# GeGLU feed-forward on one core: gate/up tiles in pairs, two plain tiles in place of four, and part of the seven-product work done in the head

## The chip, the core and the metric

The kernel runs on one core of one Trainium2 chip. The metric is the device time of one execution in microseconds (us), as a median of several executions. Each execution is fast or slow, by its time. The profile is a trace of one execution. It covers the span of that execution, from its first to its last instruction, which is 1.7 to 2.1 us shorter than the timed run. In this kernel the matmuls write to PSUM, in banks, and all other tiles lie in SBUF. A load has landed when its data are there. Engines: PE is TensorE (matmuls), PEld its weight loads, DVE is VectorE, ACT is ScalarE, POOL is GpSimd, SP is SyncE, which issues most DMAs.

## The reference

```python
B, S, D, F = 32, 32, 1024, 3584          # bf16; x has 1024 tokens
def reference(x, w_gate, w_up, w_down):
    return (gelu_tanh(x @ w_gate) * (x @ w_up)) @ w_down
```

## The kernel before

The 1024 tokens fall into two halves of 512, d_model into a front and a rear half of 512, and the 3584 features into 28 tiles of 128. Gate and up projection of a tile can be computed in two ways:

- *plain*: gate and up, two token halves, 8 matmuls each: 32 matmuls, all in bf16;
- *seven products* (Strassen-Winograd over [gate, up] and the two token halves): 7 products of 4 matmuls, so 28 matmuls. Two of the seven (a11·b11 and a12·b21, the second called P2) are bf16. The other five take sums of weights (s1 to s4, or a22 cast) and sums of x (t1 to t4, or b22 cast) in fp32r, a 32-bit type.

The kernel before computes four tiles plain, because that can start as soon as the first quarter of x and of the weights is there. It computes the other 24 with seven products, one tile at a time. GpSimd forms s1 to s4 of the next two tiles meanwhile. The down projection is a second seven-product scheme, of 392 matmuls.

```python
    # b11, b12: front half of d_model for the first, second 512 tokens; b21, b22: rear half
    FC = 2; F0 = 4                                  # four plain tiles in the head
    def acc(tag): ...                               # one PSUM bank; A 3, B 2, C 2, G 1 of them
    # [cut: loads in quarters of d_model, plain tiles for the first and then the second tokens]

        open_ft = None
        ahead = first_product(F0)                   # a11 * b11 into a bank of A, copied out ("sn1")
        for ft in range(F0, FT):                    # one tile at a time
            # [cut: start GpSimd's sums of the next pair and the loads of the one after]
            (psa, sn1), psc, psb = ahead, acc("C"), acc("B")
            prod(psc, s1, t1, True)
            sn5 = snap(psc, "sn5", 2)               # copy PSUM to SBUF on ScalarE
            # [cut: GpSimd's next sum]
            prod(psa, s2, t2, False)
            sn2 = snap(psa, "sn2", 1)
            # [cut: a22 of a later tile cast to fp32r, on ScalarE]
            if open_ft:
                last_product(open_ft)               # a22r * t4 of the tile before
            prod(psc, s4, b22r, False)
            c12 = added(sn2, psc)                   # VectorE add
            h1 = acc("G")                           # gelu's result in PSUM
            nc.scalar.activation(h1, c12, ACT.Gelu_apprx_tanh)
            prod(psb, quads(ci, fl)[1], b21, True)  # P2
            c11 = added(sn1, psb)
            h0 = ework.tile([P, NB], bf16, name="h", tag="h")
            nc.scalar.activation(h0, c11, ACT.Gelu_apprx_tanh)
            # [cut: GpSimd's next sum]
            if ft + 1 < FT:
                ahead = first_product(ft + 1)
            prod(psa, s3, t3, False)
            c22 = added(sn5, psa)
            tt(g_of(ft)[:, NB:], c22, h1, MUL)
            open_ft = (ft, psa, h0)
```

## Time and profile before

| | before |
|---|---|
| median time | 277.13 us (276.96 to 277.27, 3 runs) |
| span of the trace | 275.2 us |
| start / head / loop / down projection / tail | 4.4 / 29.0 / 149.7 / 88.4 / 3.6 us |

The page's first part (busy time and its share of the span) and its fourth (the chain of work that ended last):

```profile
PE 270.1 (98%) x1190; PEld 184.3 (67%) x1207; DVE 173.1 (63%) x184; ACT 114.4 (42%) x179; POOL 94.9 (34%) x51
...
PE 98%; issue 0%; ACT 0%
```

TensorE is busy nearly always and the chain never leaves it. But the Trainium skill warns in "Perfetto Trace Analysis", section "Identifying the Most-Contended Engine", that busy time of pipelined matmuls is a poor measure of how near the limit they run. So I look at the distance between starts. The timeline of before (start, length, engine, line, operation, tiles, count):

```profile
18.93 1.89 PE L221 MATMUL psA<-b,wg 128*128 128x512 bf16 x8
20.66 1.89 PE L221 MATMUL psB<-b,wu 128*128 128x512 bf16 x8
...
40.92 1.07 PE L268 MATMUL psA<-t,a22r 128*128 128x512 f32 x4
41.82 1.07 PE L268 MATMUL psC<-b22r,s 128*128 128x512 f32 x4
...
45.39 1.08 PE L268 MATMUL psC<-t,s 128*128 128x512 f32 x4
...
51.69 1.08 PE L268 MATMUL psC<-t,s 128*128 128x512 f32 x4
```

Eight bf16 matmuls take 20.66 - 18.93 = 1.73 us, 0.216 us each; four fp32r matmuls take 0.90 us, 0.227 us each once the starts are taken to the nanosecond. A tile of the loop should therefore need 20 × 0.227 + 8 × 0.216 = 6.27 us. The s1·t1 groups of four start at 45.39, 51.69 and 57.99 us, 6.30 us apart. So there is nothing to win in the loop but 0.03 us a tile, unless matmuls go. In what follows a loss "by starts" is the distance between two starts beyond this spacing.

The time by stretch (each row: stretch, its length, then the busy time of each engine with its instruction count, the granted clock, the DMA share and GB/s). The stretches are the head up to the first s1·t1 product, the loop up to the first matmul of the down projection, and the down projection:

```profile
core 0: us, PE busy (x) PEld busy (x) DVE busy (x) ACT busy (x) POOL busy (x), PEclk, DMA share, GB/s
4.38:33.42 29.04, 28.93 (x131) 12.82 (x132) 15.22 (x15) 9.23 (x13) 0.00 (x0) 1.00 0.89 213
33.42:183.14 149.72, 148.90 (x654) 105.74 (x665) 84.04 (x120) 82.30 (x142) 94.16 (x45) 1.00 0.29 80
183.14:271.55 88.41, 88.25 (x394) 64.12 (x396) 73.31 (x49) 20.59 (x22) 0.00 (x0) 1.00 0.51 167
```

Two groups of VectorE instructions will matter later: the multiplies by h1 (second token half, h1 in PSUM), for the two halves of the feature tiles. In such a line, after the shapes and the count, come the busy time and the mean nanoseconds of one:

```profile
L331 DVE TENSOR_TENSOR hi<-c,psG 128x512 bf16<-128x512 f32 x14 | 9.7, 690 | 1.8 <-DVE c L284 0.4
L331 DVE TENSOR_TENSOR lo<-c,psG 128x512 bf16<-128x512 f32 x10 | 6.9, 689 | 1.5 <-DVE c L284 0.5
```

### The profile page before, as it was taken

Reading aid. Unit: us, or ns where it says so; the run is one execution under the profiler, and the core shown is the slowest. Engines: PE = TensorE matmul, PEld = TensorE weight load, DVE = VectorE, ACT = ScalarE, POOL = GpSimd, SP = SyncE. Lnnn points to the kernel's source line nnn. Section 1 sums busy time; section 2 is a strip of 40 time slices with the busy share of each in tenths; the row PEclk is TensorE's granted clock in tenths of the full one; section 3 lists DMA queues with packets and bytes.
Section 4 is the critical chain, followed back from the end, with each engine's and each line's share of the span. In section 5 each row is a group of like instructions: output and inputs, shape, how many; then the busy total and the mean of one; then the engine's idle time right before and its main releaser. Section 6 shows DMA issues by size and latency. Waiting matters only on the chain.

```text
span 275.2 us, 3268 instructions
## 1 busy us (share of the span) xinstructions
PE 270.1 (98%) x1190; PEld 184.3 (67%) x1207; DVE 173.1 (63%) x184; ACT 114.4 (42%) x179; POOL 94.9 (34%) x51
## 2 busy tenths in 40 slices
PE   8999999999999999999999999999999999999995
PEld 3444467766677777777666777754447888888883
DVE  0049975555555555555555555556999999999511
ACT  4034455555555555555555555430200022972001
POOL 1000059996766749494947660000000000000000
PEclk9999999999999999999999999999999999999999
DMA  7999023150505143250508500003992245786202
GB/s 150 323 248 270 2 76 96 59 155 0 155 0 152 26 126 87 68 137 17 152 2 249 171 2 1 0 0 126 335 337 82 91 166 169 245 270 209 77 0 76
DMA packets 52192, 33.77 MB, mean 123 GB/s; under 512 B 8656, under 2 KB 52176, under 8 KB 52176
## 3 DMA queue, kind: packets, MB, share of 16 engines
q1 hardware_dynamic: 49184, 30.94, 39.1%
q10 hardware_dynamic: 2992, 2.62, 3.0%
q8 instruction: 9, 0.15, 0.2%
q14 instruction: 7, 0.06, 0.1%
HBM read 29.62 MB, written 2.10 MB: 115 GB/s over the span
## 4 chain that ended last, share of the span: by engine, by line
PE 98%; issue 0%; ACT 0%
PE psA L268 31%; PE psC L268 16%; PE psA L352 14%; PE psB L268 7%; PE psB L352 7%; PE psC L352 7%; PE psG L352 5%; PE psA L221 4%; PE psC L221 3%; PE psB L221 3%; PE psG L205 1%; PE psG L221 1%; PE tp L213 0%; ACT o_sb L491 0%; PE psG L217 0%
## 5 line engine op out<-in xcount | busy, mean ns | idle before, releaser
L268 PE MATMUL psA<-t,s 128*128 128x512 f32 x192 | 56.2, 414 | 0.0
L268 PEld LDWEIGHTS psA<-t,s 128*128 128x128 f32 x192 | 36.1, 188 | 9.4 <-ACT sn L279 0.2
L156 POOL TENSOR_TENSOR s<-wu 128x1024 fp32r<-128x1024 bf16 x11 | 23.7, 2150 | 29.3 <-PE psC L268 29.3
L284 DVE TENSOR_TENSOR c<-sn,psA 128x512 f32<-128x512 f32 x24 | 16.6, 690 | 25.4 <-PE psA L268 25.4
L268 PEld LDWEIGHTS <-wg 128*128 128x128 bf16 x192 | 16.9, 98 | 23.3 <-issue 6.3
L279 ACT COPY sn<-psA 128x512 f32<-128x512 f32 x48 | 27.8, 579 | 10.4 <-PE psA L268 10.4
L268 PE MATMUL psC<-t,s 128*128 128x512 f32 x96 | 26.1, 394 | 0.0
L268 PE MATMUL psA<-t,a22r 128*128 128x512 f32 x96 | 25.9, 391 | 0.0
L320 ACT ACTIVATE psG<-c 128x512 f32<-128x512 f32 x24 | 14.4, 602 | 27.4 <-DVE c L284 27.4
L268 PE MATMUL psC<-b22r,s 128*128 128x512 f32 x96 | 25.6, 389 | 0.0
L268 PE MATMUL psA<-b,wg 128*128 128x512 bf16 x96 | 24.6, 379 | 0.0
L158 POOL TENSOR_TENSOR s<-wg,s 128x1024 fp32r<-128x1024 bf16 x11 | 23.8, 2165 | 0.9
L157 POOL TENSOR_TENSOR s<-s,wg 128x1024 fp32r<-128x1024 f32 x11 | 23.5, 2137 | 0.9
L159 POOL TENSOR_TENSOR s<-wg,wu 128x1024 fp32r<-128x1024 bf16 x11 | 23.5, 2139 | 0.0
L268 PE MATMUL psB<-b,wg 128*128 128x512 bf16 x84 | 22.2, 381 | 0.8
L279 ACT COPY sn<-psC 128x512 f32<-128x512 f32 x24 | 14.1, 589 | 20.3 <-PE psC L268 20.3
L290 DVE TENSOR_TENSOR hi<-h,psA 128x512 bf16<-128x512 bf16 x14 | 9.6, 689 | 19.8 <-PE psA L268 19.8
L268 PEld LDWEIGHTS psC<-t,s 128*128 128x128 f32 x96 | 18.0, 188 | 4.3
L268 PEld LDWEIGHTS psA<-t,a22r 128*128 128x128 f32 x96 | 18.0, 188 | 3.8
L268 PEld LDWEIGHTS psC<-b22r,s 128*128 128x128 f32 x96 | 17.9, 188 | 3.8 <-ACT sn L279 0.2
L284 DVE TENSOR_TENSOR c<-sn,psC 128x512 f32<-128x512 f32 x24 | 16.5, 689 | 5.0 <-PE psC L268 5.0
L284 DVE TENSOR_TENSOR c<-sn,psB 128x512 f32<-128x512 f32 x24 | 16.5, 687 | 2.8
(99 smaller groups left out, 420.5 us busy)
## 6 DMA issues: line engine op xcount, KB each, us to landing
wg<-in_w_gate_dram SPq DMA_DIRECT2D x12, 512.0 KB, 4.0
wu<-in_w_up_dram SPq DMA_DIRECT2D x12, 512.0 KB, 5.2
wdb<-in_w_down_dram SPq DMA_DIRECT2D x12, 512.0 KB, 4.7
wdb<-in_w_down_dram SPq DMA_DIRECT2D x12, 384.0 KB, 4.2
v<-in_w_down_dram SPq DMA_DIRECT2D x4, 512.0 KB, 6.9
out_dram<-o_sb ACTq DMA_DIRECT2D x16, 128.0 KB, 1.7
v<-in_w_down_dram SPq DMA_DIRECT2D x4, 384.0 KB, 7.6
wg<-in_w_gate_dram SPq DMA_DIRECT2D x3, 256.0 KB, 3.9
```

Source lines behind the costliest of these rows:

```text
L156: yield eng.tensor_tensor(s1, a21, a22, ADD)
L157: yield eng.tensor_tensor(s2, s1, a11, SUB)
L158: yield eng.tensor_tensor(s4, a12, s2, SUB)
L159: yield eng.tensor_tensor(s3, a11, a21, SUB)
L205: nc.tensor.matmul(warm_ps, lhsT=ones_w, rhs=ones_m, start=True, stop=True)
L221: nc.tensor.matmul(ps, lhsT=w_tiles[0][which][:, dt, fl * P : (fl + 1) * P], rhs=x_rows(dt, nb), start=(dt == 0), stop=(dt == DT - 1),)
L268: nc.tensor.matmul(ps, lhsT=lhs[:, k, :], rhs=rhs[:, k, :], start=(start and k == 0), stop=(k == KD - 1), skip_group_check=True,)
L279: nc.scalar.copy(t, ps)
L284: tt(t, s, ps, ADD)
L290: tt(g_of(ft)[:, :NB], h0, psa, MUL)
L320: nc.scalar.activation(h1, c12, ACT.Gelu_apprx_tanh)
L352: nc.tensor.matmul(banks[m], lhsT=lhs(k)[:, m * P : (m + 1) * P], rhs=rhs(k), start=(start and k == 0), stop=(k == HF - 1), skip_group_che ...
```

## The change

The intent is to have only two plain tiles, so that 26 tiles instead of 24 use 28 matmuls in place of 32. Then the head would be too short to cover the loading of x, of the weights and the forming of t1 to t4. So ten P2 products (a12·b21) of later tiles are pulled into the head. They need nothing but the rear half of d_model for the first tokens; therefore the head works on that half first. Their results wait in SBUF, in room that the second half of the gated activations takes later. Besides, the loop now handles two tiles together, product by product.

```diff
-    F0 = 4
-    NCH = (FT - F0) // FC + 1
+    NCH = FT // FC
+    NAHEAD = 10
 ...
+        # head: first half of the reduction of 4 ahead products, then of the 2 plain tiles, ...
+        for k in range(KQ):
+            for j in range(KB):
+                product_ahead(ps[j], 0, j, k, k + 1)
+        plain0(KD, KD + KQ)
+        for j, copy in enumerate((nc.scalar.copy, nc.vector.tensor_copy) * 2):
+            product_ahead(ps[j], 0, j, KQ)
+            copy(ahead[0][:, j, :], ps[j])
+        plain0(KD + KQ, DT)
+        # [cut: loads; 4 more ahead products]
+        tt(t1, b12, b11, SUB)
+        for fl in range(FC):                       # front half of the first tokens
+            for which in (0, 1):
+                plain(tok0[fl][which], which, fl, 0, 0, KD, KD, KD - 1)
+            plain_out(fl, 0, *tok0[fl])
+        tok1 = [(acc("A"), acc("B")) for _ in range(FC)]     # second tokens
+        # [cut: their matmuls; t2, three sums; 2 more ahead products]
 ...
+            if ft < FC + NAHEAD:                   # in first_product
+                return psa, gelu(added(ahead_of(ft), psa), "h0", 4)
 ...
-        for ft in range(F0, FT):
+        for ci in range(1, NCH):                   # one pair of tiles
+            # [cut: GpSimd's sums and the loads; fts is the pair, psa its banks of A]
+            psc = [acc("C") for _ in fts]
+            for fl in range(FC):
+                prod(psc[fl], s1[fl], t1, True)
+                sn5.append(snap(psc[fl], "sn5"))
+            for fl in range(FC):
+                prod(psa[fl], s2[fl], t2, False)
+                sn2.append(snap(psa[fl], "sn2"))
+            for st in open_fts:
+                last_product(st)
+            for fl, ft in enumerate(fts):
+                prod(psc[fl], s4[fl], b22r, False)
+                h1.append(gelu(added(sn2[fl], psc[fl]), "h1", 2))    # h1 now bf16 in SBUF
+                a22r_of(ft)
+            # [cut: P2 of both tiles where it was not done ahead]
+            begun = [first_product(ft + FC) for ft in fts] if ci + 1 < NCH else []
+            for fl, ft in enumerate(fts):
+                prod(psa[fl], s3[fl], t3, False)
+                tt(g_of(ft)[:, NB:], added(sn5[fl], psa[fl]), h1[fl], MUL)
```

PSUM banks are dealt anew (A 4, B 2, C 2; G is gone).

More of the change, by code (lines that the diff above doesn't have):

```diff
@@ L68 @@
     ring = ctx.enter_context(tc.tile_pool(name="ring", bufs=4))
-    opool = ctx.enter_context(tc.tile_pool(name="osb", bufs=4))
     one = ctx.enter_context(ExitStack())
@@ L101, in g_of @@
         return by_batch(g_lo if ft < HF else g_hi)(k)
+    BANKS = {"A": 4, "B": 2, "C": 2}
     def acc(tag):
-        return ps1.tile([P, NB], fp32, name=f"ps{tag}", tag=tag, bufs={"A": 3, "B": 2, "C": 2, "G": 1}[tag])
+        return ps1.tile([P, NB], fp32, name=f"ps{tag}", tag=tag, bufs=BANKS[tag])
+    a12_ahead = [ring.tile([P, KD, KB * P], bf16, name="a12a", tag="ring") for _ in range(2)]
     b11 = xpool.tile([P, KD, NB], bf16, name="b11")
@@ L114, in x_rows, with alloc_w, load_w_all @@
         return ((b11, b12), (b21, b22))[dt // KD][nb][:, dt % KD, :]
-    w_tiles = {
-        0: tuple(
-            gpool.tile([P, DT, F0 * P], bf16, name=n, tag=f"hi{KB}", bufs=2) for n in ("wg0", "wu0")
-        )
-    }
-    def alloc_w(ci):
-        w_tiles[ci] = tuple(
-            wpool.tile([P, DT, FC * P], bf16, name=n, tag=n, bufs=b) for n, b in (("wg", 3), ("wu", 2))
+    ahead = [
+        gpool.tile([P, n, NB], fp32, name="ahead", tag=f"hi{n}", bufs=2) for n in (KB, KB, QF - KB)
+    ]
+    assert 2 * KB < NAHEAD <= KB + QF
+    w_tiles = {}
+    def alloc_w(ci, which):
+        w_tiles[ci, which] = wpool.tile(
+            [P, DT, FC * P], bf16, name=("wg", "wu")[which], tag=("wg", "wu")[which], bufs=(3, 2)[which]
         )
     def load_w(eng, ci, which, d0, d1):
-        f0, fc = (F0 + (ci - 1) * FC, FC) if ci else (0, F0)
+        f0 = ci * FC * P
         src = (wg_r, wu_r)[which]
-        eng.dma_start(out=w_tiles[ci][which][:, d0:d1, :], in_=src[:, d0:d1, f0 * P : (f0 + fc) * P])
-    def load_w_chunk(ci):
-        alloc_w(ci)
-        for which in (0, 1):
-            load_w(nc.sync, ci, which, 0, DT)
+        eng.dma_start(out=w_tiles[ci, which][:, d0:d1, :], in_=src[:, d0:d1, f0 : f0 + FC * P])
+    def load_w_all(ci, which):
+        alloc_w(ci, which)
+        load_w(nc.sync, ci, which, 0, DT)
     def quads(ci, fl=None):
         cols = slice(None) if fl is None else slice(fl * P, (fl + 1) * P)
-        wg, wu = w_tiles[ci]
+        wg, wu = w_tiles[ci, 0], w_tiles[ci, 1]
         return wg[:, :KD, cols], wg[:, KD:, cols], wu[:, :KD, cols], wu[:, KD:, cols]
-    def chunk_of(ft):
-        ci, fl = divmod(ft - F0, FC)
-        return ci + 1, fl
     s_tiles = {}
@@ L163, in a22r_of @@
     def a22r_of(ft):
-        t = spool.tile([P, KD, P], f32r, name="a22r", tag="a22r", bufs=3)
-        nc.scalar.copy(t, quads(*chunk_of(ft))[3])
+        t = spool.tile([P, KD, P], f32r, name="a22r", tag="a22r", bufs=2)
+        nc.scalar.copy(t, quads(*divmod(ft, FC))[3])
         a22rs[ft] = t
@@ L180, with load_ahead, load_w0 @@
                 out=x_nat[:, p0:p1, :],
-                in_=xf[p0 * P : p1 * P, : KQ * P].rearrange("(b p) d -> p b d", p=P),
+                in_=xf[p0 * P : p1 * P, KD * P : (KD + KQ) * P].rearrange("(b p) d -> p b d", p=P),
             )
-        for dt in range(KQ):
-            load_w((nc.sync, nc.scalar)[dt % 2], 0, 0, dt, dt + 1)
-        load_w(nc.scalar, 0, 1, 0, KQ)
+        alloc_w(0, 0)
+        alloc_w(0, 1)
+        def load_ahead(i, k0, k1):
+            f0, n = FC + i * KB, min(KB, NAHEAD - i * KB)
+            nc.sync.dma_start(
+                out=a12_ahead[i][:, k0:k1, : n * P],
+                in_=wg_r[:, KD + k0 : KD + k1, f0 * P : (f0 + n) * P],
+            )
+        def load_w0(eng, d0, d1):
+            for which in (0, 1):
+                load_w(eng, 0, which, d0, d1)
         def load_xT(nb, d0, d1):
@@ L191, in load_xT @@
             )
-        for q in range(1, 4):
-            d0, d1 = q * KQ, (q + 1) * KQ
-            load_xT(0, d0, d1)
-            load_w(nc.sync, 0, 0, d0, d1)
-            load_w(nc.sync, 0, 1, d0, d1)
+        for k in range(KQ):
+            load_ahead(0, k, k + 1)
+        load_w0(nc.scalar, KD, KD + KQ)
+        load_xT(0, KD + KQ, DT)
+        load_ahead(0, KQ, KD)
+        load_w0(nc.sync, KD + KQ, DT)
+        load_ahead(1, 0, KD)
+        load_xT(0, 0, KD)
+        load_w0(nc.sync, 0, KD)
         load_xT(1, 0, KD)
         load_xT(1, KD, DT)
-        load_w_chunk(1)
-        load_w_chunk(2)
-        warm_ps = acc("G")
+        warm_ps = acc("A")
         for _ in range(NWARM):
             nc.tensor.matmul(warm_ps, lhsT=ones_w, rhs=ones_m, start=True, stop=True)
-        tags = iter("CCAB")
+        tags = iter("CCBB")
         for dt in range(KQ):
@@ L210 @@
                 tag = next(tags)
-                tp = ps1.tile([P, hw], bf16, name="tp", tag=tag, bufs={"A": 3, "B": 2, "C": 2}[tag])
+                tp = ps1.tile([P, hw], bf16, name="tp", tag=tag, bufs=BANKS[tag])
                 for b in range(HALF):
@@ L215, with plain @@
                     )
-                (nc.vector.tensor_copy, nc.scalar.copy)[half](b11[:, dt, half * hw : (half + 1) * hw], tp)
+                (nc.vector.tensor_copy, nc.scalar.copy)[half](b21[:, dt, half * hw : (half + 1) * hw], tp)
         nc.tensor.matmul(warm_ps[:, : NB // 2], lhsT=ones_w, rhs=ones_m[:, : NB // 2], start=True, stop=True)
-        def plain(ps, which, fl, nb, d0, d1):
+        def plain(ps, which, fl, nb, d0, d1, first=0, last=DT - 1):
             for dt in range(d0, d1):
@@ L222, in plain, with gelu @@
                     ps,
-                    lhsT=w_tiles[0][which][:, dt, fl * P : (fl + 1) * P],
+                    lhsT=w_tiles[0, which][:, dt, fl * P : (fl + 1) * P],
                     rhs=x_rows(dt, nb),
-                    start=(dt == 0),
-                    stop=(dt == DT - 1),
-                )
+                    start=(dt == first),
+                    stop=(dt == last),
+                )
+        def gelu(src, tag, bufs):
+            h = ework.tile([P, NB], bf16, name=tag, tag=tag, bufs=bufs)
+            nc.scalar.activation(h, src, ACT.Gelu_apprx_tanh)
+            return h
         def plain_out(ft, nb, gate, up):
-            h = ework.tile([P, NB], bf16, name="h", tag="h")
-            nc.scalar.activation(h, gate, ACT.Gelu_apprx_tanh)
-            tt(g_of(ft)[:, nb * NB : (nb + 1) * NB], h, up, MUL)
-        head = [(acc(a), acc(b)) for a, b in ("AB", "AB", "AC", "CG")]
-        for q in range(3):
-            for which in (0, 1):
-                for dt in range(q * KQ, (q + 1) * KQ):
-                    for fl in range(F0):
-                        plain(head[fl][which], which, fl, 0, dt, dt + 1)
-        for fl in range(F0):
-            for which in (0, 1):
-                plain(head[fl][which], which, fl, 0, 3 * KQ, DT)
-            plain_out(fl, 0, *head[fl])
-        chunk1 = sums(1, nc.vector)
-        tt(t1, b12, b11, SUB)
-        after = (
-            lambda: (next(chunk1), tt(t2, b22, t1, SUB)),
-            lambda: (next(chunk1), next(chunk1)),
-            lambda: (tt(t3, b22, b12, SUB), a22r_of(F0)),
-            lambda: (next(chunk1), a22r_of(F0 + 1)),
-        )
-        for fl, (a, b) in enumerate(("AB", "AB", "AC", "AC")):
-            ps = acc(a), acc(b)
-            for which in (0, 1):
-                plain(ps[which], which, fl, 1, 0, DT)
-            if fl == 1:
-                nc.scalar.copy(b22r, b22)
-            plain_out(fl, 1, *ps)
-            after[fl]()
-        tt(t4, b21, t2, SUB)
-        g_hi = g_tiles("hi", bf16, N)
-        nc.gpsimd.tensor_copy(ident[:, :1], t4[:, 0, :1])
+            tt(g_of(ft)[:, nb * NB : (nb + 1) * NB], gelu(gate, "h0", 4), up, MUL)
         def prod(ps, lhs, rhs, start):
@@ L275, in prod, with ahead_of, product_ahead @@
                 )
-        def snap(ps, tag, bufs):
-            t = ework.tile([P, NB], fp32, name=tag, tag=tag, bufs=bufs)
-            nc.scalar.copy(t, ps)
-            return t
+        def ahead_of(ft):
+            i, j = divmod(ft - FC, KB)
+            return ahead[i][:, j, :]
+        def product_ahead(ps, i, j, k0=0, k1=KD):
+            for k in range(k0, k1):
+                nc.tensor.matmul(
+                    ps,
+                    lhsT=a12_ahead[i][:, k, j * P : (j + 1) * P],
+                    rhs=b21[:, k, :],
+                    start=(k == 0),
+                    stop=(k == KD - 1),
+                )
@@ new lines, with plain0 @@
+        ps = [acc(t) for t in "CCAA"]
+        tok0 = [(acc("A"), acc("B")) for _ in range(FC)]
+        def plain0(d0, d1):
+            for which in (0, 1):
+                for dt in range(d0, d1):
+                    for fl in range(FC):
+                        plain(tok0[fl][which], which, fl, 0, dt, dt + 1, KD, KD - 1)
+        for k in range(KQ):
+            for j in range(KB):
[4 more added lines that the diff above has]
+            copy(ahead[0][:, j, :], ps[j])
@@ new lines @@
+        plain0(KD + KQ, DT)
+        a12_ahead.append(ring.tile([P, KD, KB * P], bf16, name="a12a", tag="ring"))
+        load_w_all(1, 1)
+        load_w_all(1, 0)
+        load_ahead(2, 0, KD)
+        load_w_all(2, 0)
+        for j, tag in enumerate("CCAA"):
+            ps = acc(tag)
+            product_ahead(ps, 1, j)
+            (nc.scalar.copy, nc.vector.tensor_copy)[j % 2](ahead[1][:, j, :], ps)
+        tt(t1, b12, b11, SUB)
+        for fl in range(FC):
+            for which in (0, 1):
+                plain(tok0[fl][which], which, fl, 0, 0, KD, KD, KD - 1)
+            plain_out(fl, 0, *tok0[fl])
@@ new lines @@
+        tok1 = [(acc("A"), acc("B")) for _ in range(FC)]
+        for fl in range(FC):
+            for which in (0, 1):
+                plain(tok1[fl][which], which, fl, 1, 0, KD)
+        tt(t2, b22, t1, SUB)
+        nc.scalar.copy(b22r, b22)
+        chunk1 = sums(1, nc.vector)
+        for _ in range(3):
+            next(chunk1)
+        for fl in range(FC):
+            for which in (0, 1):
+                plain(tok1[fl][which], which, fl, 1, KD, DT)
+            plain_out(fl, 1, *tok1[fl])
@@ L282, in added @@
+        load_w_all(2, 1)
+        for j, tag in enumerate("CC"):
+            ps = acc(tag)
+            product_ahead(ps, 2, j)
+            nc.scalar.copy(ahead[2][:, j, :], ps)
         def added(s, ps):
@@ L285, in added, with snap, first_product @@
             return t
+        def snap(ps, tag):
+            t = ework.tile([P, NB], fp32, name=tag, tag=tag, bufs=2)
+            nc.scalar.copy(t, ps)
+            return t
+        def first_product(ft):
+            psa = acc("A")
+            prod(psa, quads(*divmod(ft, FC))[0], b11, True)
+            if ft < FC + NAHEAD:
+                return psa, gelu(added(ahead_of(ft), psa), "h0", 4)
+            return psa, snap(psa, "sn1")
         def last_product(st):
@@ L290, in last_product @@
             tt(g_of(ft)[:, :NB], h0, psa, MUL)
-        def first_product(ft):
-            psa = acc("A")
-            prod(psa, quads(*chunk_of(ft))[0], b11, True)
-            return psa, snap(psa, "sn1", 2)
-        open_ft = None
-        ahead = first_product(F0)
-        for ft in range(F0, FT):
-            ci, fl = chunk_of(ft)
-            fs = slice(fl * P, (fl + 1) * P)
-            if fl == 0:
-                nxt = sums(ci + 1, nc.gpsimd) if ci + 1 < NCH else iter(())
-                if ci + 2 < NCH:
-                    load_w_chunk(ci + 2)
-            s1, s2, s3, s4 = (s[:, :, fs] for s in s_tiles[ci])
-            (psa, sn1), psc, psb = ahead, acc("C"), acc("B")
-            prod(psc, s1, t1, True)
-            sn5 = snap(psc, "sn5", 2)
-            next(nxt, None)
-            prod(psa, s2, t2, False)
-            sn2 = snap(psa, "sn2", 1)
-            if ft + FC < FT:
-                a22r_of(ft + FC)
-            if open_ft:
-                last_product(open_ft)
-            prod(psc, s4, b22r, False)
-            c12 = added(sn2, psc)
-            h1 = acc("G")
-            nc.scalar.activation(h1, c12, ACT.Gelu_apprx_tanh)
-            prod(psb, quads(ci, fl)[1], b21, True)
-            c11 = added(sn1, psb)
-            h0 = ework.tile([P, NB], bf16, name="h", tag="h")
-            nc.scalar.activation(h0, c11, ACT.Gelu_apprx_tanh)
-            next(nxt, None)
-            if ft + 1 < FT:
-                ahead = first_product(ft + 1)
-            prod(psa, s3, t3, False)
-            c22 = added(sn5, psa)
-            tt(g_of(ft)[:, NB:], c22, h1, MUL)
-            open_ft = (ft, psa, h0)
@@ new lines @@
+        tt(t3, b22, b12, SUB)
+        begun = [first_product(FC + fl) for fl in range(FC)]
+        next(chunk1)
+        tt(t4, b21, t2, SUB)
+        nc.gpsimd.tensor_copy(ident[:, :1], t4[:, 0, :1])
+        open_fts = []
+        for ci in range(1, NCH):
+            fts = range(ci * FC, (ci + 1) * FC)
+            if fts[0] == HF:
+                g_hi = g_tiles("hi", bf16, N)
+            if ci + 1 < NCH:
+                if ci + 2 < NCH:
+                    load_w_all(ci + 2, 0)
+                for _ in sums(ci + 1, nc.gpsimd):
+                    pass
+            s1, s2, s3, s4 = ([s[:, :, fl * P : (fl + 1) * P] for fl in range(FC)] for s in s_tiles[ci])
+            sn5, sn2, h1, h0 = [], [], [], []
+            psa, first = zip(*begun)
+            psc = [acc("C") for _ in fts]
+            for fl in range(FC):
+                prod(psc[fl], s1[fl], t1, True)
+                sn5.append(snap(psc[fl], "sn5"))
+            for fl in range(FC):
+                prod(psa[fl], s2[fl], t2, False)
[6 more added lines that the diff above has]
+                a22r_of(ft)
+            if ci + 2 < NCH:
+                load_w_all(ci + 2, 1)
+            if fts[0] < FC + NAHEAD:
+                h0 = first
+            else:
+                for fl in range(FC):
+                    psb = acc("B")
+                    prod(psb, quads(ci, fl)[1], b21, True)
+                    h0.append(gelu(added(first[fl], psb), "h0", 4))
+            begun = [first_product(ft + FC) for ft in fts] if ci + 1 < NCH else []
+            for fl, ft in enumerate(fts):
+                prod(psa[fl], s3[fl], t3, False)
+                tt(g_of(ft)[:, NB:], added(sn5[fl], psa[fl]), h1[fl], MUL)
+            open_fts = list(zip(fts, psa, h0))
@@ L375 @@
         p2_b21 = by_batch([load_b(LO, 0, b) for b in range(NBT)])
-        bankb = [acc(t) for t in "BCBC"]
+        bankb = [acc(t) for t in "CCBB"]
         span(bankb, by_batch(A12), p2_b21, 0, KB, False, True)
-        last_product(open_ft)
+        for st in open_fts:
+            last_product(st)
         span(bankb, by_batch(A12), p2_b21, KB, HF)
@@ L398, in store @@
         def store(m, tok, col, in0, in1):
-            o = opool.tile([P, NB], bf16, name="o_sb", tag="o_sb")
+            o = late.tile([P, NB], bf16, name="o_sb", tag="o_sb", bufs=MT)
             tt(o, in0, in1, ADD)
@@ L416 @@
         sb = snaps(bankb, "snb")
-        banka = [acc(t) for t in "AAAG"]
+        banka = [acc("A") for _ in range(MT)]
         product(banka, by_batch(A11), by_batch(v11), True)
@@ L488 @@
         for m in range(MT):
-            o = opool.tile([P, NB], bf16, name="o_sb", tag="o_sb")
+            o = late.tile([P, NB], bf16, name="o_sb", tag="o_sb", bufs=MT)
             r0 = NB + m * P
```

## The prediction

> **What bounds it now.** TensorE: the page gives PE 98% busy, and the chain of waits is PE for 98% of the span. Busy times of pipelined matmuls overlap, so I read spacing from the timeline: four a22r matmuls start at 40.92 us and the next group at 41.82, 0.227 us per fp32r matmul; eight bf16 head matmuls start at 18.93, the next at 20.66, 0.216 us. (The Trainium skill, "TensorE: Matmul & The Clock Gate", section "Back-to-back issue gap", gives N/2.4 + 2.5 = 216 ns for 512 columns: this trace agrees for bf16.) From the timeline: start 4.4 us; head to 32.5 (128 matmuls, 28.15 us against 27.65 at 0.216); Strassen loop to 183.1 (24 tiles of 28 matmuls, 6.30 us a tile); down projection to 271.5; tail 3.7. The loop shows no waits: 20 x 0.227 + 8 x 0.216 = 6.27. So pairing, which lengthens the distance to every PSUM reader, removes no wait there, because none exists.
>
> **What the change does.** Two tiles move from plain (32 matmuls each) to seven-product form (28): 8 of 1192 matmuls go. In bf16 48 go (10.37 us), in fp32r 40 come (9.07 us): net -1.3 us. Ten P2 products move into the head: the same work earlier, at the cost of PSUM copies off the critical path. Pairs halve the bf16-to-fp32r switches; a tile costs 0.03 to 0.04 us over the pure sum, so about -0.5 us in all. The down projection keeps its matmuls; one more last product (0.9 us), counted above, falls inside it. GpSimd's sums (4 x 2.15 = 8.6 us a pair) still fit, though a pair without P2 lasts only 48 matmuls = 10.8 us instead of 12.6.
>
> **Head.** DMA demand is about the same: 2 MB of weights and all of x by the second tokens. Before, 256 KB landed about every 0.7 to 0.9 us. At that rate I estimate the second pack of ahead weights at 10.8 us (needed 12.0), the front half of x and w0 at 14.5 (needed 15.4), the second tokens at 16.7 and 18.7 (needed 19 and 22.4). VectorE is tight: t1 to t4 (2.29 us each) and four sums (1.22). I estimate t4 finished at 35.1 us, GpSimd's first s1 at 37.5 and s2 at 39.7, needed at 38.4 and 40.2; the adds of the first two ahead tiles end 0.3 us before s2*t2 needs them. A late transpose would turn this into a stall of 0.5 to 2 us once. I allow 0.4 us.
>
> **Sum.** -1.3 - 0.5 + 0.4 = -1.4 us: **275.7 us**, range 274.9 to 277.6 (8 in 10). Chances: faster by over 2% 0.02, within 2% 0.95, slower by over 2% 0.03.
>
> **Right if:** PE spacing unchanged; chunks with P2 done ahead 10.8 us, later ones 12.5 us; the first fp32r product at about 29.1 us instead of 33.4; down projection from about 180.2 us instead of 183.1, lasting 0.9 us longer; VectorE and ScalarE less busy in the loop without effect on the span.
>
> **Wrong if:** PE gaps over 1 us at the loop's first or second chunk (waiting for GpSimd's sums or VectorE's adds), at the front half of the first tokens (transposed x, now one large transfer), or early in the down projection (its sums start 0.9 us later; before, they had some 3 us to spare). The biggest risk is the head's DMA order: w0 comes in rows of 512 bytes instead of 1024. A gain over 2 us would mean that before's head lost more than I read.

## The result and the profile after

The changed kernel was timed in three batches, each beside the kernel before on the same chip. A ratio is the mean time of its fast runs over that of the other kernel's fast runs in the same rounds, so it is not quite the ratio of the medians.

| batch | changed kernel, median | before, median | ratio, 95% interval |
|---|---|---|---|
| first result | 275.66 us (275.09 to 276.45) | 277.04 us | 0.9956 (0.9935 to 0.9977) |
| with the experiments on the parts ("after_again") | 275.48 us (275.20 to 276.24) | 276.99 us | 0.9949 (0.9937 to 0.9961) |
| with the last experiments ("after_base") | 275.85 us (275.35 to 276.52) | 276.94 us | 0.9963 (0.9947 to 0.9978) |

It is 1.1 to 1.5 us faster, about 0.45%, where 1.4 us were predicted. The page after, same two parts:

```profile
PE 269.1 (98%) x1199; PEld 187.9 (69%) x1199; DVE 195.9 (72%) x194; ACT 111.9 (41%) x183; POOL 107.3 (39%) x55
...
PE 91%; SPq 5%; DMA 2%; issue 0%; DVE 0%; ACT 0%; DVEq 0%
```

TensorE still bounds it. The new 5% of SPq and 2% of DMA in the chain lie in the head: the chain there runs through the issue and landing of the transposed x. VectorE is busy 22.8 us *longer* than before. The stretches after, with the same borders:

```profile
core 0: us, PE busy (x) PEld busy (x) DVE busy (x) ACT busy (x) POOL busy (x), PEclk, DMA share, GB/s
4.71:29.28 24.57, 24.32 (x112) 10.77 (x112) 15.03 (x15) 9.37 (x13) 0.00 (x0) 1.00 0.99 238
29.28:180.63 151.35, 151.35 (x675) 110.74 (x673) 105.87 (x128) 80.30 (x146) 106.55 (x49) 1.00 0.32 89
180.63:269.93 89.30, 89.30 (x400) 64.86 (x400) 74.51 (x52) 19.97 (x21) 0.00 (x0) 1.00 0.51 165
```

Head -4.47, loop +1.63, down projection +0.89 us: -1.95 us from the first to the last useful matmul. The first useful matmul starts 0.33 us later and the tail is 0.2 us longer, which leaves 1.4 us of the span. The 0.89 us of the down projection is one more last product inside it: 4 × 0.227 = 0.91. The timeline shows the old spacing:

```profile
26.02 1.89 PE L264 MATMUL psC<-b,a12a 128*128 128x512 bf16 x8
27.74 1.89 PE L249 MATMUL psA<-b,wg 128*128 128x512 bf16 x8
...
42.16 1.98 PE L249 MATMUL psA<-t,a22r 128*128 128x512 f32 x8
43.98 1.98 PE L249 MATMUL psC<-b22r,s 128*128 128x512 f32 x8
...
49.37 1.98 PE L249 MATMUL psC<-t,s 128*128 128x512 f32 x8
...
60.20 1.98 PE L249 MATMUL psC<-t,s 128*128 128x512 f32 x8
```

(27.74 - 26.02) / 8 = 0.215 and (43.98 - 42.16) / 8 = 0.2275 us. Pairs with P2 done ahead start 10.83 us apart (60.20 - 49.37), later ones 12.56 us.

The multiplies by h1, before 0.69 us each:

```profile
L391 DVE TENSOR_TENSOR lo<-c,h 128x512 bf16<-128x512 f32 x12 | 19.2, 1602 | 0.6
L391 DVE TENSOR_TENSOR hi<-c,h 128x512 bf16<-128x512 f32 x14 | 16.2, 1160 | 0.5
```

And one wait of TensorE in the head, in the timeline after. The note in brackets is the idle time of the engine before the group, and what ended it:

```profile
17.03 2.29 DVE L299 TENSOR_TENSOR t<-b,b 128x2048 fp32r<-128x2048 bf16 x1 [0.80 <-DMA b<-in_x_dram]
...
18.80 1.03 PE L231 MATMUL psA<-b,wg 128*128 128x512 bf16 x4
...
19.24 1.28 DVE L245 TENSOR_TENSOR lo<-h,psB 128x512 bf16<-128x512 bf16 x2
...
19.98 1.02 PE L231 MATMUL psB<-b,wu 128*128 128x512 bf16 x4 [0.15 <-DVE lo L245]
```

Four matmuls from 18.80 should be followed at 19.66. The next group starts at 19.98: its PSUM bank is freed by the multiply of 19.24, which stands in VectorE's queue behind t1, and t1 waited for the transposed x. The bracket shows 0.15 us only, because it counts from the modelled end of the group before (18.80 + 1.03 = 19.83); by starts 0.32 us is lost.

### The profile page after: what moved, and what is told of

It is laid out like the page before. It is cut to its first block, busy times and chain, and to the rows that moved or that the text cites. A ratio compares the mean times of both kernels' runs of the same rounds, so it can differ in the third digit from the quotient of the medians.

```text
span 273.7 us, 3347 instructions
## 1 busy us (share of the span) xinstructions
PE 269.1 (98%) x1199; PEld 187.9 (69%) x1199; DVE 195.9 (72%) x194; ACT 111.9 (41%) x183; POOL 107.3 (39%) x55
## 4 chain that ended last, share of the span: by engine, by line
PE 91%; SPq 5%; DMA 2%; issue 0%; DVE 0%; ACT 0%; DVEq 0%
PE psA L249 34%; PE psA L412 18%; PE psC L249 17%; PE psC L412 7%; PE psB L412 7%; PE psB L249 5%; SPq L197 3%; DMA b<-in_x_dram 2%; PE psB L231 1%; PE psA L231 1%; SPq L134 1%; SPq L186 1%; PE psC L264 1%; DVE lo L245 0%; ACT o_sb L552 0%
## 5 line engine op out<-in xcount | busy, mean ns | idle before, releaser
L249 PE MATMUL psA<-t,s 128*128 128x512 f32 x208 | 54.1, 402 | 0.0
L241 ACT ACTIVATE h<-c 128x512 bf16<-128x512 f32 x52 | 31.8, 628 | 37.2 <-DVE c L326 37.2
L249 PEld LDWEIGHTS psA<-t,s 128*128 128x128 f32 x208 | 39.1, 188 | 9.2
L154 POOL TENSOR_TENSOR s<-wu 128x1024 fp32r<-128x1024 bf16 x12 | 26.4, 2202 | 25.0 <-DMA wu<-in_w_up_dram 18.3
L155 POOL TENSOR_TENSOR s<-s,wg 128x1024 fp32r<-128x1024 f32 x12 | 27.8, 2313 | 0.9
L156 POOL TENSOR_TENSOR s<-wg,s 128x1024 fp32r<-128x1024 bf16 x12 | 26.3, 2188 | 0.9
L157 POOL TENSOR_TENSOR s<-wg,wu 128x1024 fp32r<-128x1024 bf16 x12 | 26.6, 2213 | 0.0
L331 ACT COPY sn<-psA 128x512 f32<-128x512 f32 x42 | 23.6, 585 | 6.8 <-PE psA L249 6.8
L249 PEld LDWEIGHTS psC<-t,s 128*128 128x128 f32 x104 | 19.5, 188 | 4.2
L249 PEld LDWEIGHTS psA<-t,a22r 128*128 128x128 f32 x104 | 19.5, 188 | 4.1
L249 PEld LDWEIGHTS psC<-b22r,s 128*128 128x128 f32 x104 | 19.5, 188 | 4.1
L326 DVE TENSOR_TENSOR c<-sn,psC 128x512 f32<-128x512 f32 x26 | 17.9, 689 | 5.3 <-PE psC L249 5.3
L391 DVE TENSOR_TENSOR lo<-c,h 128x512 bf16<-128x512 f32 x12 | 19.2, 1602 | 0.6
L455 ACT COPY snb<-psC 128x512 f32<-128x512 f32 x4 | 2.2, 590 | 36.5 <-PE psC L412 36.5
```

The lines of the kernel that those rows point to most:

```text
L154: yield eng.tensor_tensor(s1, a21, a22, ADD)
L155: yield eng.tensor_tensor(s2, s1, a11, SUB)
L156: yield eng.tensor_tensor(s4, a12, s2, SUB)
L157: yield eng.tensor_tensor(s3, a11, a21, SUB)
L241: nc.scalar.activation(h, src, ACT.Gelu_apprx_tanh)
L249: nc.tensor.matmul(ps, lhsT=lhs[:, k, :], rhs=rhs[:, k, :], start=(start and k == 0), stop=(k == KD - 1), skip_group_check=True,)
```

## The experiments

Theory: the gain is the matmuls that go, net of the dearer fp32r (-1.3 us), and fewer switches from bf16 to fp32r (-0.5 us), less some waiting in the head; the products ahead make it possible to have two plain tiles, and earn nothing by themselves. Rivals: the pairing is the cause, or a better-fed head is.

### after_again: the changed kernel unchanged, a base

> The changed kernel unchanged, as the base for the others of this batch. Expected 0.4 to 0.6% faster than the kernel before (about 275.6 us). The first useful matmul began at 4.71 us in its first profile against 4.38 before, because the untransposed x landed 0.3 us later: if that belongs to the change it shows again; if it is chance of one execution the start comes back near 4.4.

Measured: 275.48 us, ratio 0.9949. The late start showed again in this trace (first useful matmul at 4.69 us), but not in the third trace of the same kernel (4.38 us); its variants lie anywhere from 4.29 to 4.79, and before_h1_sbuf, which has the head of the kernel before, at 4.64. So it varies from execution to execution in both kernels, and isn't shown to be a cost of the change. The head's wait was 1.21 us this time.

### four_plain and four_plain_mended: the two tiles put back into plain form

```diff
+    PLAIN = 2                                   # chunks of two tiles
-        for ci in range(1, NCH):
+        for ci in range(PLAIN, NCH):
+        for fl in range(FC):                    # in the head, after the last ahead products
+            for nb in range(2):
+                gate, up = acc("A"), acc("B")
+                plain(gate, 0, fl, nb, 0, DT, ci=1)
+                plain(up, 1, fl, nb, 0, DT, ci=1)
+                plain_out(FC + fl, nb, gate, up)
+                # mended: t3 after the first of these; then one sum after each
```

> The changed kernel with four plain tiles instead of two: pairs and the ten products ahead stay, only the two tiles that the change moved into seven-product form go back (64 plain bf16 matmuls for 40 fp32r and 16 bf16). My theory (the gain is mostly the 8 matmuls fewer, net of the fp32r surcharge): 64 x 0.216 - 40 x 0.227 - 16 x 0.216 = +1.3 us over the changed kernel, so about 276.9 us, with 8 matmuls more in the trace. Rival (the gain is a better-fed head or the pairing): it stays within 0.3 us of the changed kernel.

Measured: 278.71 us, ratio 1.0061, 3.2 us over the changed kernel of its batch. The trace showed a fault of my own: 1.2 us of TensorE waiting at 45 us for the first ahead sums, queued behind t3. So the run says nothing of the two tiles.

> Four plain tiles once more, with the fault of the first try taken out: there VectorE formed t3 just ahead of the first two ahead sums, and TensorE waited 1.2 us for those at 45 us; t3 now comes five microseconds earlier. My theory: without that wait the kernel is 1.3 us slower than the changed kernel (about 276.9 us, ratio to before near 1.000), with no gap of TensorE over 0.6 us after 10 us. If the two tiles in seven-product form were worth the 3.2 us that the first try showed, it stays near 278.5.

Measured: 277.60 us, ratio 1.0030 (1.0018 to 1.0043). The stretches of its trace:

```profile
4.58:43.62 39.04, 38.77 (x174) 17.35 (x176) 17.71 (x19) 11.84 (x17) 0.00 (x0) 1.00 0.69 165
43.62:182.41 138.79, 138.13 (x607) 101.74 (x617) 96.90 (x118) 73.97 (x134) 98.01 (x45) 1.00 0.33 93
182.41:271.71 89.30, 89.19 (x398) 64.88 (x400) 74.61 (x52) 19.96 (x21) 0.00 (x0) 1.00 0.51 165
```

The loop is 151.35 - 138.79 = 12.56 us shorter for one pair fewer, and 64 plain matmuls at 0.216 are worth 13.82 us in the head: +1.26 us, the predicted term. From first to last useful matmul this trace has 267.13 us. The three traces of the changed kernel have 265.22, 265.94 and 266.51, mean 265.89: a difference of 1.24. That this agrees so well is partly luck. The trace of the variant begins with five slow matmuls (1.0 us), and two of the three traces of the changed kernel caught the slowest execution of their batch (276.24 and 276.52 us). In time the variant is 0.7 to 0.8% slower by the ratios, some 1.8 to 2.2 us (the changed kernel wasn't timed in this batch, and each ratio is uncertain by 0.3 to 0.6 us), so 0.5 us or more of it isn't accounted for by this term. About 0.25 us of that lies outside the span: timed run less span is 2.0 us in every run of both four_plain kernels, and 1.8 in the changed kernel. The rest stays open. "Within 0.3 us of the changed kernel", which the rivals needed, is ruled out.

### pairs_only: the kernel before with the pair loop alone

The run takes from the changed kernel what the pair loop needs: its PSUM banks, h1 in SBUF, the place of the loads in the loop.

```diff
-        for ft in range(F0, FT):                 # one tile at a time, h1 in PSUM
+        for ci in range(1, NCH):                 # the changed kernel's pair loop, h1 in SBUF,
+            ...                                  # P2 of both tiles always in the loop
-    bufs={"A": 3, "B": 2, "C": 2, "G": 1}
+    bufs={"A": 4, "B": 2, "C": 2}
```

> The kernel before with the pair loop alone: four plain tiles and its old head, no product ahead, h1 kept in SBUF instead of PSUM as in the changed kernel. My theory: pairing removes no wait, it only halves the bf16-to-fp32r switches, worth 0.4 to 0.5 us over the loop: chunk period 12.56 us instead of 12.60, whole kernel 0.0 to 0.3% faster than before. Rival (pairing is the cause of the gain): 1.4 us faster, the same as the changed kernel.

Measured: 276.38 us, ratio 0.9973 (0.9961 to 0.9985). The s1·t1 groups of eight start 12.56 us apart:

```profile
45.31 1.98 PE L269 MATMUL psC<-t,s 128*128 128x512 f32 x8
...
57.87 1.98 PE L269 MATMUL psC<-t,s 128*128 128x512 f32 x8
```

Before, two tiles took 2 × 6.30 = 12.60. From first to last useful matmul it needs 266.67 us against 267.16, 0.49 less, with the same matmuls. No run took switches alone away, but the starts in the traces, to the nanosecond, show where the time is. Far from a switch the matmuls keep to 215.8 and 226.7 ns, in before, after and pairs_only alike. The switch from bf16 to fp32r, the six gaps after it, and the switch back with the gap after it take 40 ns more than that in all. This comes once in every tile of before and once in every pair here: 12 times less, 0.48 us. No other spacing in the loop differs. Pairing is about half of the gain of this batch (0.27 of 0.51%), not all of it. The other half, 0.24% or 0.7 us (uncertain by 0.5), is what two plain tiles less and the products ahead bring together: the 1.26 us of the matmuls, less what head, start and tail give back.

### no_ahead: two plain tiles without the products ahead

```diff
-    NAHEAD = 10
+    NAHEAD = 0
-        # all loads, matmuls and copies of the products ahead
```

> The changed kernel without the products ahead: two plain tiles, pairs, every P2 in the loop; the same matmuls in number and type. If P2 ahead is only a rearrangement of the same work, the time stays at the changed kernel's. My theory: it is what covers the loading of x and the sums that the first fp32r product needs; without it I estimate from the landings of the changed kernel's trace (second tokens at 19.1 us with 1 MB of ahead weights before them, so about 16 without) that the first fp32r product starts at 23.7 us where 20.6 would be free of waits: +3 us (1.5 to 5), slower than the kernel before.

Measured: 278.62 us, ratio 1.0060 (1.0047 to 1.0072): 3.1 us slower than the changed kernel of its batch, where 3 were expected, and slower than before. The timeline shows where TensorE stands in the head:

```profile
6.51 1.04 PE L222 MATMUL psB<-b,wu 128*128 128x512 bf16 x4 [0.94 <-DMA wu<-in_w_up_dram]
...
10.55 1.04 PE L222 MATMUL psA<-b,wg 128*128 128x512 bf16 x4 [1.27 <-DMA wg<-in_w_gate_dram]
...
16.49 1.02 PE L222 MATMUL psB<-b,wu 128*128 128x512 bf16 x4 [1.40 <-DVE lo L236]
```

By starts, 1.1, 1.4 and 1.6 us are lost there: twice to loads, once to the bank behind t1. So the ten products earn nothing as work (they are the same matmuls elsewhere), but without them, and with the loads ordered as here, the two tiles cost more than they save.

### sum_in_psum and before_h1_sbuf: why VectorE became slower

```diff
 # sum_in_psum, on the changed kernel
-                tt(g_of(ft)[:, NB:], added(sn5[fl], psa[fl]), h1[fl], MUL)
+                c22 = acc("B")
+                tt(c22, sn5[fl], psa[fl], ADD)
+                tt(g_of(ft)[:, NB:], c22, h1[fl], MUL)
 # before_h1_sbuf, on the kernel before
-            h1 = acc("G")
+            h1 = ework.tile([P, NB], bf16, name="h1", tag="h1", bufs=2)
```

> The changed kernel with the sum c22 written to a free PSUM bank of tag B instead of SBUF, so that the following multiply by h1 again reads one operand from PSUM and one from SBUF, as before the change. Theory: the multiplies took 0.69 to 2.65 us in the changed kernel because both operands came from SBUF while GpSimd was working; they return to 0.69 us, VectorE's busy time falls by about 20 us (196 to about 177) and GpSimd's adds return from 2.2 to 2.15 us. The time doesn't change (within 0.3 us of the changed kernel), since the loop's pitch was already that of TensorE. Rival 1 (type or tile cause it, not memory): they stay at 1.4 us. Rival 2 (VectorE is on the path): the time falls by 0.5 us or more.

> The kernel before with one thing of the change alone: h1 in SBUF as bf16 instead of PSUM as fp32. Theory: its multiply by c22 then has two SBUF operands and waits for GpSimd's adds: from 0.69 us to between 1.0 and 1.8 us on average, VectorE's busy time up by 8 to 25 us; the time stays within 0.3% of before, with the loop at 6.30 us a tile.

Measured with the sum in PSUM: the multiplies are back at 0.69 us, VectorE's busy time fell from 195.9 to 178.9 us, GpSimd's from 107.3 to 103.5. The groups:

```profile
L393 DVE TENSOR_TENSOR hi<-psB,h 128x512 bf16<-128x512 f32 x14 | 9.7, 692 | 1.0
L393 DVE TENSOR_TENSOR lo<-psB,h 128x512 bf16<-128x512 f32 x12 | 8.3, 692 | 0.9
```

Measured in the kernel before with h1 alone in SBUF:

```profile
L331 DVE TENSOR_TENSOR lo<-c,h 128x512 bf16<-128x512 f32 x10 | 13.7, 1375 | 1.4 <-DVE c L284 0.5
L331 DVE TENSOR_TENSOR hi<-c,h 128x512 bf16<-128x512 f32 x14 | 12.9, 920 | 1.8 <-DVE c L284 0.5
```

VectorE's total there went from 173.1 to 182.6 us. So it is the memory of the operands: with both in SBUF the multiply is slow, with one in PSUM it isn't. (h1 stayed bf16 in the first of these runs, so it isn't the type.) The timeline of the changed kernel shows the partner:

```profile
60.23 2.15 POOL L157 TENSOR_TENSOR s<-wg,wu 128x1024 fp32r<-128x1024 bf16 x1
60.28 2.65 DVE L391 TENSOR_TENSOR lo<-c,h 128x512 bf16<-128x512 f32 x1
```

GpSimd's add began 0.05 us before the multiply and ended at 62.38; the multiply ended at 62.93, 0.55 us after that. Of the 26 multiplies, the ten that overlapped no GpSimd add took 0.69 us each; of the 16 others, 13 took 0.92 to 2.65 us. This is what the Trainium skill states ("SBUF — State Buffer", section "Who interferes with whom"): a VectorE instruction with two SBUF inputs contends with a GpSimd instruction that reads SBUF; with at most one SBUF input, and outside VectorE's two-port modes, it doesn't. This agrees in both directions: up to 2.65 us with two, 0.69 us with one.

Did it cost time? The loop of the changed kernel takes 151.35 us with the slow multiplies and 151.35 with the fast ones, so no: VectorE has the room. Whole runs: sum_in_psum 276.24 us, ratio 0.9971 (0.9958 to 0.9984), which is no faster than the changed kernel (not timed in this batch) and outside the 0.3 us that I expected; 0.3 us of it lies in a longer tail (4.12 against 3.82 us); before_h1_sbuf 277.32 us, ratio 1.0007 (0.9988 to 1.0026), the same as before.

### t1_later and k1_on_act: two tries at the head

```diff
 # t1_later
-        tt(t1, b12, b11, SUB)
         for fl in range(FC):
             ...
             plain_out(fl, 0, *tok0[fl])
+            if fl == 0:
+                tt(t1, b12, b11, SUB)
 # k1_on_act
-            load_ahead(0, k, k + 1)
+            load_ahead(0, k, k + 1, (nc.sync, nc.scalar)[k])
```

> The changed kernel with t1 formed after the first multiply of the first tokens instead of before both. In two traces TensorE lost 0.3 and 1.2 us at about 19.5 us, because the PSUM bank of the second tokens' up product was freed by a multiply queued behind t1, which waited for the transposed x (landed 16.9 and 17.6 us). Theory: that wait goes, 0.3 to 1.2 us in the trace, median 0.3 to 0.8 us faster than the changed kernel (about 275.0); the chain of t2 and the sums moves 0.5 us later and may give back up to 0.4 us at the first s2 product.

Measured: 276.06 us (274.84 to 277.09), ratio 0.9967 (0.9944 to 0.9989): not faster. The wait at 19.5 us was gone in the trace, but the last ahead weights came late in this execution (0.86 us lost at 26 us), and the s2 product, which needs sums at the end of VectorE's queue, waited some 0.6 us. A miss: what moves VectorE's queue back comes out again at its end.

> The changed kernel with the second of the first two ahead weight loads issued from ScalarE's queue ahead of w0, as the kernel before had its second weight row. In the traces of the changed kernel this row landed at 5.6 to 5.8 us and TensorE waited 0.26 us for it or not at all. Theory: the wait for it goes, and the first useful matmul stays at about 4.7 us; 0 to 0.4 us faster. If the late start (4.7 against 4.4 us) comes from what is loaded beside x, the start moves too; it then has to land x_nat before 3.5 us.

Measured: 275.45 us (275.13 to 276.61), ratio 0.9954 (0.9940 to 0.9967), the same as the changed kernel. The second row of ahead weights landed at 4.3 us and wasn't waited for; w0, pushed back, landed at 7.8 us and was (0.7 us). The start moved to 4.51 us, x having landed at 3.3.

### after_base, tok1_in_c and tok1_in_c_sum_psum: the wait for the bank taken away

```diff
-        tok1 = [(acc("A"), acc("B")) for _ in range(FC)]
+        tok1 = [(acc("A"), acc("C")) for _ in range(FC)]
-        for j, tag in enumerate("CC"):           # the last two ahead products
+        for j, tag in enumerate("BB"):
```

> The changed kernel once more, as the base of this batch: 0.4 to 0.6% faster than before. In its trace a TensorE wait at about 19 us of 0 to 1.2 us, longer the later t1 starts: from six traces so far, t1 starting at 16.7, 17.0, 17.4 and 17.7 us went with waits of 0, 0.3, 0.6 and 1.2.

Measured: 275.85 us, ratio 0.9963. Its trace has the longest wait of all, 1.41 us by starts:

```profile
18.02 2.29 DVE L299 TENSOR_TENSOR t<-b,b 128x2048 fp32r<-128x2048 bf16 x1 [1.90 <-DMA b<-in_x_dram]
18.68 1.03 PE L231 MATMUL psA<-b,wg 128*128 128x512 bf16 x4
20.23 1.28 DVE L245 TENSOR_TENSOR lo<-h,psB 128x512 bf16<-128x512 bf16 x2
20.96 0.81 PE L231 MATMUL psB<-b,wu 128*128 128x512 bf16 x3 [1.25 <-DVE lo L245]
```

The same queue of loads landed the transposed x at 16.9, 17.6 and 17.9 us in the three traces of this kernel, and the wait was 0.32, 1.21 and 1.41 us. The later x, the longer the wait.

> The changed kernel with the up products of the second tokens in the idle PSUM banks of tag C (and the last two ahead products in those of tag B): their first matmul no longer needs a bank that the multiply behind t1 frees. No instruction moves. Theory: the TensorE wait at 19 us is gone wherever the transposed x lands, and the sums behind t1 come no later, so 0.3 to 1.0 us faster than the base, and the spread of its times shrinks. Rival: the late transpose only moves the wait to the first s2 product (which needs the ahead sums behind t3), and the time stays.

Measured: 275.92 us (275.58 to 276.19), ratio 0.9963 (0.9949 to 0.9978): the same as the base. In its trace the wait is gone:

```profile
19.58 1.03 PE L231 MATMUL psA<-b,wg 128*128 128x512 bf16 x4
20.44 1.03 PE L231 MATMUL psC<-b,wu 128*128 128x512 bf16 x4
```

but x landed early in this execution (16.6 us), and k1_on_act, with the old banks and x at the same 16.6 us, shows no wait there either; so the trace doesn't show what the banks do for a late x; and the first five useful matmuls came 0.38 to 0.43 us apart, at half speed, which cost 1.0 us. The spread of its times, 0.6 us, is smaller than the base's 1.2, as expected; the median didn't move. Why the median did not follow isn't settled.

> The same with c22 in PSUM too. Theory (VectorE is off the path of the loop): within 0.3 us of the run with the banks alone; its multiplies 0.69 us each. If the 0.5 us by which the run with c22 in PSUM came out above the changed kernel's was real and not the batch, it is 0.5 us slower again.

Measured: 275.82 us, ratio 0.9963 (0.9949 to 0.9978), multiplies at 0.69 us: the same as the run with the banks alone (x landed early again, at 16.5 us). So the 0.5 us by which sum_in_psum had come out higher didn't repeat. The longer tail did (4.12 us). No variant beat the changed kernel by more than the spread.

## Why the prediction was right, and where it was not

- **The bound, right.** TensorE's spacing (0.216 and 0.227 us) was read before and is the same after.
- **The matmuls that go, -1.3 us, right.** Shown by putting them back: the loop got 12.56 us shorter, the 64 plain matmuls at the unchanged spacing are 13.82 us, and the time rose. It rose by 0.5 us or more beyond this; of that 0.25 us lies outside the span, and the rest stays open.
- **Pairing, -0.5 us, right in size.** Alone it gave 0.49 us in the trace and 0.27% of the time. That it takes away no wait is shown by the loop of before, 6.30 us against 6.27. That the switches are what it saves is read from the starts: 40 ns around each, 12 fewer of them in pairs_only. No run changed the switches alone.
- **The products ahead, right.** They are rearranged work; without them the time rises by 3.1 us.
- **Chunks (pairs) of 10.8 and 12.5 us, down projection 0.9 us longer, first fp32r product at 29.1 us, right.** Measured: 10.83, 12.56, 0.89, and 29.28 in the first trace (29.98 and 30.26 in the two others). The down projection began at 180.63 us there, where 180.2 was predicted.
- **The head's allowance, "I allow 0.4 us", in the right place only in part.** The prediction looked for a stall at the loop's first chunks or at the front half of the first tokens. The wait came at the up products of the second tokens, by way of a PSUM bank that a multiply behind t1 frees, and had 0.32, 1.21 and 1.41 us in three traces. The cause that it named, a late transposed x with a tight VectorE, was the right one. By starts, the head of the changed kernel lost 0.6, 1.3 and 1.9 us in all in its three traces (the first includes a load wait of 0.26 us, the third 0.5 us of slow first matmuls), mean 1.25; the head of before lost 0.7, mainly in its first matmuls at half speed. The difference of 0.5 us is near the allowance, by another way than foreseen, and partly by luck: two of the three traces are of the slowest execution of their batch. In the trace of the first result the head lost no more than before (0.6 against 0.7); there the 0.4 us came from a start 0.33 us later and a tail 0.2 us longer, which the prediction doesn't name.
- **"VectorE and ScalarE less busy in the loop without effect on the span": the first half wrong for VectorE.** I counted instructions at their old durations and passed over h1's move from PSUM to SBUF. VectorE's busy time in the loop rose from 84.0 to 105.9 us; the multiplies by h1 went from 0.69 to 1.36 us on average ((19.2 + 16.2) / 26), which is some 17 of these 22 us. ScalarE fell, 82.3 to 80.3 us. "Without effect on the span" held: the loop is equally long without the contention.

## What to carry to other kernels

When TensorE is at its pitch, price a change as matmuls times spacing for each type, and ask of everything else only whether it makes TensorE wait. Work that needs few inputs is worth pulling to the front even when it saves nothing by itself: it pays for what then needs no filler. And when a change deals PSUM banks anew, check which VectorE instructions now have both inputs in SBUF while GpSimd works; here they cost VectorE some 17 us and the kernel nothing.

## What the Trainium skill lacked or had wrong

- "TensorE: Matmul & The Clock Gate", section "Back-to-back issue gap": it gives about 131 ns per matmul of 512 columns as the sustained figure in a real kernel, and says that N/2.4 + 2.5 ns (216 ns) over-counts there. Here long streams of weight load and matmul ran at 216 ns in bf16; the formula, which the prediction used, is right, and no stream ran at 131 ns. (Other parts of the page have the figure right.)
- The same page gives no spacing for fp32r: 227 ns here, with weight loads of 188 ns against 98 in bf16, and 0.04 us lost around each change between the two types.
- The same page, section "Part 1: The HAM clock gate (the "warmup" mystery)", calls the number of slow matmuls at the start variable from run to run. It is: with the same six warm-up matmuls ahead, useful matmuls at about 427 ns numbered none to five, 0 to 1.0 us of the time.
- "SBUF — State Buffer", section "Who interferes with whom", is right about two SBUF inputs, but has no figure for how long it makes a tensor_tensor: a multiply of 0.69 us took up to 2.65 us, and GpSimd's adds of 2.15 us up to 2.60.
- No page tells how far the landing of a load moves between executions: the same transposed load, with the same queue ahead of it, was issued between 11.6 and 12.4 us and landed between 16.9 and 17.9 us in three traces of the changed kernel.
- No page tells of the time from the landing of the last DMA to the program's own last instruction: 0.85 us in the kernel before, 1.07 in the changed one (in all three traces) and 1.38 with the sum in PSUM. What sets it wasn't found.
